# Eight small sums of a gated MLP's second pass, moved from VectorE to GpSimd

## The chip, the cores and the metric

The kernel runs on one core of a Trainium2 chip. Five engines work beside each other on that core: TensorE (PE in the profile) multiplies matrices, VectorE (DVE) and GpSimd (POOL) do sums of tiles, ScalarE (ACT) does copies, casts and the Gelu, and SyncE (SP) issues the transfers between HBM and the on-chip memory. Products are built up in eight banks of PSUM; POOL works only on SBUF here, so everything that reads a bank is DVE's or ACT's. The metric is the device time of one execution in microseconds (us), lower is better; several executions are timed, and their median counts.

## The reference

```
def reference(x, w_gate, w_up, w_down):
    g = jnp.einsum("bsd,df->bsf", x, w_gate)
    u = jnp.einsum("bsd,df->bsf", x, w_up)
    h = _gelu(g) * u
    return jnp.einsum("bsf,fd->bsd", h, w_down)
```

`_gelu` is the tanh form. x is 1 x 2048 x 1024, the two weights in front 1024 x 3584, the last 3584 x 1024, all in bf16.

## The kernel before

The 2048 rows of x are done in two passes (`ip` 0 and 1) of 1024 rows, which are two chunks of 512. A pass has two halves: the units, which make h from x, w_gate and w_up, and then `down` (line 515), which multiplies h by w_down.

**Units.** Each of the 14 units covers 256 columns of w_gate and w_up. A plain product would have eight blocks for each weight (two chunks of rows, two halves of the inner 1024, two halves of the 256 columns). The kernel does it in seven, by a scheme of Winograd's, with sums of blocks of x (`t1` to `t4`, four tiles each, with `tb` a cast; `make_t`, line 157) and sums of blocks of the weights (`s1` to `s4`, two tiles each; `make_s`, line 162). The sums of x are made once a pass, the sums of the weights for every unit. Two of the seven products need no sums and are called raw: `raw_products` (line 199) puts one into the banks `e`, copies it out with ACT (`p1`) and puts the other into the banks `c`. `finish_raw` (209) adds both on DVE (`add`, 204: first the gate part into a tile `sum`, then the up part in its bank), takes the Gelu on ACT, and multiplies the two on DVE into `hT`. The rest of a unit (`unit`, 213) is four products with sums, s2 by t2, s1 by t1, s3 by t3 and s4 by tb, and for units that are not `apart` a seventh, whole one (`whole_p4`).

**The divided product.** For pairs of units that `SPLIT` (line 47) names, the seventh product, with T4, is done for both units together, and the same scheme is applied to it once more (`split_p4`, 267). This needs sums of sums: `split_sums` (167) makes four tiles from the weights of both units, and `inner_sums_t` (256) makes n1 to n4 from the tiles of T4. Each n has two halves, so `inner_sums_t` issues eight instructions of 128 x 256, and they serve all divided pairs of a pass. In the first pass the first divided pair is units 4 and 5, and the n are made on GpSimd in unit 4 (`FIRST_N`, line 718). In the second pass it is units 0 and 1, and the n are first read at the end of unit 1.

**The boundary between the passes.** While the first pass's `down` runs, `more` (807) puts in the work that the second pass needs first, by steps: at step 50 the weights of units 0 and 1 are loaded, at step 58 DVE makes the sums of unit 0's weights, at step 62 it makes the sums of x and, behind them, the n. Then the second pass begins with the raw products of units 0 and 1, and both use the same pair of banks `K` for their second part, so unit 1's must wait until unit 0's has been read:

```
                raw_of(0, Ea, K)()
                raw_of(1, Eb, K)()
```

**What sets the order.** DVE, GpSimd, TensorE and SyncE do their work in the order in which the program names it (`manual_schedule`), in the units ScalarE too. An instruction that waits therefore holds all that stand behind it on its engine. Within a unit, `prepare` (713) is called behind the s1 product; it gives GpSimd its work: `split_sums` for the pair in its second unit, then the sums of the next unit's weights. Tiles of 2 KB a partition live in a pool of 52 slots (`SLOTS`); a new tile takes the slot that came free first, and the instruction that writes it waits until the former tile there has been read. Weights have three buffers of their own (`wpool`), so the load of unit u + 2 (`loaded`, called in `aside(0)`) waits until the last reader of unit u - 1's weights, among them `split_sums`, is done.

Of the kernel before, what the change touches and what calls it, by code (L numbers as in the profile page):

```python
# [10 lines left out]
def kernel(  # L11
# [60 lines left out]
    def slot(shape, dtype, name):  # L72
        return kpool.tile(shape, dtype, name=name, tag="k")
# [64 lines left out]
    def sums_s(w, eng):  # L138
        GU = range(2)
        sh = [P, KH, P]  # L140
        a11, a21 = [[w[:, i, :KH, h : h + P] for i in GU] for h in (0, P)]
        a12, a22 = [[w[:, i, KH:, h : h + P] for i in GU] for h in (0, P)]
        return Sums(
            how={
                "s1": lambda q, GU=GU: [new(eng, a21[i], a22[i], ADD, "s1", sh) for i in GU],
                "s2": lambda q: [new(eng, q["s1"][i], a11[i], SUB, "s2", sh) for i in GU],
                "s3": lambda q: [new(eng, a11[i], a21[i], SUB, "s3", sh) for i in GU],
                "s4": lambda q: [new(eng, a12[i], q["s2"][i], SUB, "s4", sh) for i in GU],
                "sa": lambda q: [cast(a22[i], "sa", sh) for i in GU],
                "sh": lambda q: cast(w[:, :, KH + 2 :, P:], "sh", [P, 2, 2, P]),  # L150
            }
        )
# [51 lines left out]
    def add(ps, other):  # L204
        g = new(dve, ps[0], other[0], ADD, "sum", dtype=f32)
        dve(ps[1], ps[1], other[1], ADD)
        return g, ps[1]
# [48 lines left out]
    def inner_sums_t(t, eng):  # L256
        n = t["n"] = [slot([P, 2, Q], f32r, "n") for _ in range(4)]
        left, right = slice(0, Q), slice(Q, N)
        for k in range(2):
            b1, b2 = t["t4"][k], t["t4"][2 + k]  # L260
            n1, n2, n3, n4 = [x[:, k] for x in n]
            eng(n1, b1[:, right], b1[:, left], SUB)
            eng(n2, b2[:, right], n1, SUB)
            eng(n3, b2[:, right], b1[:, right], SUB)
            eng(n4, b2[:, left], n2, SUB)
# [379 lines left out]
    s, t = sums_s(w, dve), sums_t(xT)  # L645
# [45 lines left out]
    def raw_of(u, e, c):  # L691
        p1 = raw_products(e, c, xT, loaded(u))
        return lambda: finish_raw(u, c, p1)

    def apart(u):
        return u - u % 2 in SPLIT[ip]

    for ip in range(NPASS):
        with tc.manual_schedule(engines={ENG.Activation}):
            if ip == 0:  # L700
                ws = {1: w, 2: ahead}
                late = lambda: add(cc, nxt["p1"])
            else:
                raw_of(0, Ea, K)()
                raw_of(1, Eb, K)()
            for u in range(1 if ip == 0 else 0, NU):
                js = making(u) if ip == 0 else []
                first = (ip, u) == (0, 1)
                odd_u = u % 2 == 1
                if first or not odd_u:  # L710
                    halves = {}

                def prepare():
                    if first:
                        pool_behind(t["t4"][-1])
                    if ip == 0 and (u >= NU - 2 or not apart(u)):
                        fetch_wd(making(u + 1))
                    if (ip, u) == (0, FIRST_N):
                        inner_sums_t(t, pool)
                    if odd_u and apart(u):  # L720
                        halves["sums"] = split_sums(ws[u - 1], ws[u])
                    if u + 1 < NU:
                        nxt["s"] = make_s(
                            loaded(u + 1), pool, () if apart(u) or apart(u + 1) else ("sa",)
                        )
                    if apart(u) and odd_u:
                        halves["sh"] = sums_s(ws[u], pool)["how"]["sh"](None)
                    if len(js) == 1:
                        store_made(js[0])
                    for j in js[1:]:  # L730
                        keep_whole(j)

                def keep(part, ps):
                    if js:
                        keep_part(js[0], part, ps)

                def aside(part):
                    if first and part < 0:
                        rest_of_0(part + 2)
                    if part == 0 and ip == 0 and apart(u) and u < NU - 2:  # L740
                        fetch_wd(making(u + 1))
                    if part == 0 and u + 2 < NU:
                        loaded(u + 2)
                    if part == 0 and "t4" not in t:
                        t.make("t4")
                    if part == 1:
                        if apart(u) and not odd_u and u + 1 < NU:
                            halves["sa"] = sums_s(ws[u], pool)["how"]["sa"](None)

                def mid():  # L750
                    if not apart(u) and "sa" not in s:
                        s.make("sa")

                def ahead():
                    if odd_u and u + 1 < NU:
                        raw_of(u + 1, Ea, D)()
                        nxt["c11"] = raw_of(u + 2, K, D)

                def behind():
                    if "c11" in nxt:  # L760
                        nxt.pop("c11")()

                def p4(c12):
                    if not (odd_u and apart(u)):
                        times(2 * u, 1, gelu(c12[0]), c12[1])
                    if first:
                        whole_p4(u, odd, s, t, after_first, behind)
                    elif not apart(u):
                        whole_p4(u, (Ea, Eb)[odd_u], s, t, ahead, behind)
                    elif odd_u:  # L770
                        rest = split_p4(
                            u - 1, Ea, Eb, *D, halves["sa"], halves["sh"], halves["sums"], t, c12
                        )
                        if u + 1 < NU:
                            p1 = raw_first(K, xT, loaded(u + 1)), raw_first(
                                D, xT, loaded(u + 2)
                            )
                            rest()
                            for n, c in enumerate((Ea, Eb)):
                                raw_second(c, xT, loaded(u + 1 + n))  # L780
                                finish_raw(u + 1 + n, c, p1[n])
                        else:
                            rest()

                def after_first():
                    raw_of(2, even, cc)()
                    nxt["c11"] = raw_of(3, dd, cc)

                if first:
                    banks = odd, cc, dd  # L790
                else:
                    banks = (Eb, D, K) if odd_u else (Ea, K, D)
                unit(
                    u, banks, s, t, late if first else None, prepare, aside, keep,
                    mid, p4,
                )
                if odd_u and not first and u + 1 < NU:
                    if not apart(u):
                        Ea, Eb, K, D = Ea, K, D, Eb
                    else:  # L800
                        Ea, Eb, K, D = K, D, Eb, Ea
                s = nxt.pop("s", None)

        last = ip == NPASS - 1
        got, nxt = {}, {}

        def more(step):
            if last:
                return
            if step in (-1, 0, 2):  # L810
                store_made({-1: NJ - 3, 0: NJ - 2, 2: NJ - 1}[step])
            if step == 0:
                xT[:] = new_x()
            if step >= 24 and step % 2 == 0 and step // 2 - 12 < len(moves):
                c, ko = moves[step // 2 - 12]
                transposing(xT, c, ko, (2 * (ip + 1) + c) * N)
            if step == 50:
                ws.clear()
                ws.update({n: load_w(n) for n in range(2)})
            if step == 58:  # L820
                got["s"] = make_s(ws[0], dve)
            if step == 62:
                got["t"] = make_t(xT)
                inner_sums_t(got["t"], dve)

        down(ip, Ea + D, K + Eb, last, more)
        Ea, Eb, K, D = K, Ea, Eb, D
        if not last:
            t, s = got["t"], got["s"]
# [29 lines left out]
```

## Time and profile before

| | us |
|---|---|
| median of three runs (541.38 to 542.25) | 542.18 |
| the profiled execution, its time | 542.75 |
| the profiled execution, its span | 541.0 |
| TensorE busy, share of the span | 98% |
| VectorE busy | 395.6 (73%) |
| GpSimd busy | 310.2 (57%) |
| ScalarE busy | 268.0 (50%) |
| eight n on VectorE, second pass (first start to last start) | 272.0 to 279.1 |
| eight n on GpSimd, first pass (first start to last start) | 57.7 to 62.8 |

All positions are microseconds from the span's start. The second pass begins near 271.7. In the profile nearly all sums of VectorE carry line 80 and those of GpSimd line 83, since two helpers record them; matmuls carry line 101. So one goes by the names of tiles: `n<-t` is an n made from T4. Matmuls are pipelined, so TensorE counts as busy also where it runs below its peak, and a row of the granted clock has to be read beside it. A bracket at the end of a line of the timeline gives the idle time of the engine just before, and what ended it.

### The profile page before, as it was taken

What the parts mean: (1) busy time and instruction counts of PE and PEld (TensorE: products, weight loads), DVE (VectorE), ACT (ScalarE), POOL (GpSimd) and SP (SyncE); (2) the same over time, 40 slices, a digit from 0 to 9 for tenths busy, and PEclk for the clock granted to TensorE, in tenths of its full rate; (3) what the DMA queues carried; (4) which work ended last, traced back from release to release, by engine and by line L of the source; (5) the groups of instructions that cost most, each with busy time, mean ns of one, the idle gap of its engine ahead of it and who ended that gap; (6) DMA issues with size and microseconds to landing.
All of it is one profiled execution on the core that took longest, in us unless ns stands there. A gap on an engine that the chain in (4) does not pass through costs nothing.

```text
span 541.0 us, 7973 instructions
## 1 busy us (share of the span) xinstructions
PE 531.6 (98%) x2550; PEld 387.7 (72%) x2571; DVE 395.6 (73%) x604; ACT 268.0 (50%) x479; POOL 310.2 (57%) x291
## 2 busy tenths in 40 slices
PE   8999999999999999999979999999999999999997
PEld 4568686868677646888838686867777685478887
DVE  2986777887887895695884857676766759979844
ACT  3557476767676410264335565566565561113340
POOL 1179999889898200000088898989898900000194
PEclk9999999999999999999989999999999999999999
DMA  9685556748483899979643250505052039662752
GB/s 243 161 219 171 181 156 194 225 127 264 129 266 126 288 390 316 265 182 274 225 118 84 72 138 19 157 1 155 8 150 59 22 110 386 223 233 84 241 172 69
DMA packets 108202, 93.34 MB, mean 173 GB/s; under 512 B 17280, under 2 KB 93056, under 8 KB 108160
## 3 DMA queue, kind: packets, MB, share of 16 engines
q1 hardware_dynamic: 108160, 92.82, 58.0%
q8 instruction: 21, 0.34, 0.3%
q14 instruction: 21, 0.17, 0.1%
HBM read 74.45 MB, written 15.20 MB: 166 GB/s over the span
## 4 chain that ended last, share of the span: by engine, by line
PE 93%; DMA 4%; DVE 2%; issue 1%; SPq 0%; DVEq 0%
PE bank L101 92%; DMA q<-td 2%; DVE n L80 1%; DMA xn<-in_x_dram 1%; DVE t L80 1%; DMA out_dram<-st 1%; SPq L587 0%; SPq L362 0%; DVE st L80 0%; PE bank L594 0%; DVE sum L80 0%; DVEq L80 0%; SPq L466 0%
## 5 line engine op out<-in xcount | busy, mean ns | idle before, releaser
L83 POOL TENSOR_TENSOR s<-w 128x512 fp32r<-128x512 bf16 x122 | 142.0, 1181 | 123.0 <-PE bank L101 103.2
L101 PE MATMUL bank<-t,s 128*128 128x512 f32 (+1 forms) x688 | 160.7, 387 | 0.0
L101 PEld LDWEIGHTS bank<-t,s 128*128 128x128 f32 x688 | 127.5, 188 | 26.7 <-issue 0.3
L101 PE MATMUL bank<-xT,w 128*128 128x512 bf16 (+1 forms) x489 | 110.3, 380 | 4.0 <-DVE sum L80 3.1
L179 ACT ACTIVATE g<-sum 128x512 f32<-128x512 f32 x101 | 63.9, 633 | 74.7 <-DVE sum L80 74.2
L80 DVE TENSOR_TENSOR hT<-g,bank 128x512 bf16<-128x512 f32 x112 | 76.6, 687 | 27.2 <-ACT g L179 20.5
L101 PEld LDWEIGHTS <-w 128*128 128x128 bf16 x504 | 48.5, 99 | 60.1 <-issue 5.8
L97 ACT COPY p<-bank 128x512 f32<-128x512 f32 x124 | 69.1, 588 | 39.2 <-PE bank L101 38.7
L83 POOL TENSOR_TENSOR s<-s,w 128x512 fp32r<-128x512 f32 x60 | 69.1, 1170 | 2.3 <-ACT g L179 1.4
L83 POOL TENSOR_TENSOR s<-w,s 128x512 fp32r<-128x512 bf16 x60 | 69.3, 1175 | 0.0
L80 DVE TENSOR_TENSOR sum<-bank,p 128x512 f32<-128x512 f32 x54 | 37.1, 687 | 41.1 <-PE bank L101 40.7
L83 POOL TENSOR_TENSOR q<-q 128x256 fp32r<-128x256 f32 x28 | 21.0, 781 | 78.7 <-DMA raw<-in_w_down_dram 77.5
L101 PE MATMUL bank<-q 128*128 128x512 f32 x240 | 58.9, 389 | 0.0
L101 PE MATMUL bank<-tb,s 128*128 128x512 f32 x216 | 53.7, 390 | 0.2
L101 PEld LDWEIGHTS bank<-q 128*128 128x128 f32 x240 | 45.0, 188 | 9.3
L101 PE MATMUL bank<-raw,hT 128*128 128x512 bf16 x218 | 48.4, 379 | 0.3
L92 ACT CAST tb<-raw 128x512 fp32r<-128x512 bf16 x28 | 17.1, 624 | 61.4 <-DMA raw<-in_w_down_dram 27.7
L101 PEld LDWEIGHTS bank<-tb,s 128*128 128x128 f32 x216 | 40.3, 188 | 9.5 <-POOL s L83 1.2
L80 DVE TENSOR_TENSOR q<-hT 128x512 fp32r<-128x512 bf16 x56 | 39.0, 696 | 5.6 <-PE bank L101 5.6
L97 ACT COPY u<-bank 128x512 f32<-128x512 f32 x62 | 34.1, 585 | 15.0 <-PE bank L101 15.0
L80 DVE TENSOR_TENSOR bank<-bank,p 128x512 f32<-128x512 f32 x54 | 37.5, 694 | 4.9 <-PE bank L101 4.3
L101 PEld LDWEIGHTS <-hT 128*128 128x128 bf16 x224 | 21.8, 98 | 26.5 <-issue 0.5
(77 smaller groups left out, 581.9 us busy)
## 6 DMA issues: line engine op xcount, KB each, us to landing
raw<-in_w_down_dram SPq DMA_DIRECT2D x76, 256.0 KB, 4.2
q<-td SPq DMA_DIRECT2D x60, 256.0 KB, 4.6
w<-in_w_gate_dram SPq DMA_DIRECT2D x27, 512.0 KB, 4.2
w<-in_w_up_dram SPq DMA_DIRECT2D x27, 512.0 KB, 5.4
td<-m SPq DMA_DIRECT2D x12, 768.0 KB, 5.4
w<-td SPq DMA_DIRECT2D x6, 1024.0 KB, 10.1
out_dram<-st SPq DMA_DIRECT2D x32, 128.0 KB, 1.7
td<-w SPq DMA_DIRECT2D x2, 768.0 KB, 6.3
```

Of the source, the lines that this page charges most:

```text
L80: nc.vector.tensor_tensor(out=out, in0=a, in1=b, op=op)
L83: nc.gpsimd.tensor_tensor(out=out, in0=a, in1=b, op=op)
L92: nc.scalar.copy(out=t, in_=src)
L97: nc.scalar.copy(out=t, in_=ps)
L101: nc.tensor.matmul(ps, lhsT=lhs, rhs=rhs, start=start, stop=stop, skip_group_check=True)
L179: nc.scalar.activation(g, src, ACT.Gelu_apprx_tanh)
```

## The change

The eight sums n of the second pass are issued in another place and on another engine. They are no longer given to VectorE at step 62 of the first `down`, behind the sums of x, but to GpSimd in unit 0 of the second pass, behind its sums of unit 1's weights. The instructions, their shapes and their operands stay the same, and so does the first pass.

```diff
@@ -723,6 +723,8 @@
                         nxt["s"] = make_s(
                             loaded(u + 1), pool, () if apart(u) or apart(u + 1) else ("sa",)
                         )
+                    if (ip, u) == (1, 0):
+                        inner_sums_t(t, pool)
                     if apart(u) and odd_u:
                         halves["sh"] = sums_s(ws[u], pool)["how"]["sh"](None)
                     if len(js) == 1:
@@ -821,7 +823,6 @@
                 got["s"] = make_s(ws[0], dve)
             if step == 62:
                 got["t"] = make_t(xT)
-                inner_sums_t(got["t"], dve)
```

## Prediction

> **What bounds the kernel now.** The page comes first: TensorE (PE) is busy 98% of the span and holds 93% of the chain that ended last. So only a place where PE stands still, or runs slower than it could, is worth anything. The chain in order of time shows where it leaves PE; its columns are start, length, what:
>
> ```profile
> 270.76 1.29 DVE t L80 x2
> 272.05 0.34 DVE n L80
> 272.42 5.15 DVE n L80 x4
> 277.59 1.32 DVE n L80 x2
> ...
> 279.52 0.61 DVE sum L80
> 280.17 21.76 PE bank L101 x101
> ```
>
> These are the eight n sums of the change, and one `sum` behind them that PE waits for. The timeline of the same stretch says what PE was doing, and for how long each n ran (start, length, engine, line, operation; idle time before it in brackets):
>
> ```profile
> 271.69 5.35 PE L101 MATMUL bank<-xT,w 128*128 128x512 bf16 x23
> ...
> 276.19 1.37 DVE L80 TENSOR_TENSOR n<-t 128x256 fp32r<-128x256 f32 x1
> 277.24 1.33 POOL L83 TENSOR_TENSOR s<-w 128x512 fp32r<-128x512 bf16 x1
> 277.59 1.25 DVE L80 TENSOR_TENSOR n<-t,n 128x256 fp32r<-128x256 f32 x1
> 278.77 0.41 DVE L80 TENSOR_TENSOR n<-t,t 128x256 fp32r<-128x256 f32 x1
> 279.11 0.41 DVE L80 TENSOR_TENSOR n<-t,n 128x256 fp32r<-128x256 f32 x1
> 279.44 0.68 DVE L80 TENSOR_TENSOR sum<-bank,p 128x512 f32<-128x512 f32 x1
> ...
> 280.17 3.49 PE L101 MATMUL bank<-xT,w 128*128 128x512 bf16 x8 [3.13 <-DVE sum L80]
> ...
> 283.10 6.14 PE L101 MATMUL bank<-t,s 128*128 128x512 f32 x24
> ```
>
> The 24 matmuls from 271.69 are unit 0's two raw products and unit 1's first. The next eight, unit 1's second product, write the banks K that `sum` (the first `add` of unit 0) and the product `hT` must read first. `sum` was ready when PE had filled the bank near 274.4, but stood in VectorE's (DVE's) queue behind the n sums until 279.44. An n takes 0.41 us when GpSimd (POOL) is still, and 1.25 to 1.37 while POOL makes unit 1's sums. The table by stretches shows what the stop does afterwards (length, then busy time of PE, PEld, DVE, ACT, POOL, then PE's granted clock, DMA share and GB/s):
>
> ```profile
> 277.00:280.20 3.20, 0.07 (x2) 0.03 (x1) 3.17 (x6) 0.05 (x1) 1.57 (x3) 1.00 0.63 159
> 280.20:283.70 3.50, 3.50 (x9) 1.56 (x9) 1.90 (x3) 2.17 (x4) 3.40 (x3) 0.51 0.02 5
> 283.70:290.00 6.30, 6.30 (x29) 5.15 (x29) 2.75 (x4) 3.18 (x6) 3.32 (x3) 1.00 0.00 0
> ```
>
> After standing still PE runs 3.5 us at half clock. Last, POOL's and PE's later rows, for what the moved work will meet:
>
> ```profile
> 281.31 2.29 POOL L83 TENSOR_TENSOR s<-w,s 128x512 fp32r<-128x512 bf16 x2
> 286.60 1.17 POOL L83 TENSOR_TENSOR s<-w 128x512 fp32r<-128x512 bf16 x1 [3.00 <-PE bank L101]
> ...
> 290.10 1.18 POOL L83 TENSOR_TENSOR s<-w,s 128x512 fp32r<-128x512 bf16 x1
> 291.24 2.30 POOL L83 TENSOR_TENSOR s<-w 128x512 fp32r<-128x512 bf16 x2
> ```
>
> **The change part by part.** *Removed from DVE: eight n sums,* 271.96 to 279.44, 7.5 us. What it is worth is read at PE, as three terms. (1) The stop: the last of the 24 matmuls starts at 276.66, and such matmuls start 0.21 us apart (32 of them from 301.54 to 308.27), so the next could start at 276.87 in place of 280.17: 3.30 us. (2) Eight at half clock: 280.17 to 283.10 is 2.93, at full clock 8 x 0.21 = 1.70: 1.23 us. (3) The start of unit 0's 24: 283.10 to the next group at 289.08 is 5.98, against 290.89 to 296.33 = 5.44 for the same 24 in unit 1: 0.54 us. Sum 5.07 us. Behind 289.08 the chain is PE without a break, so the gain keeps.
>
> [...]
>
> *What is late next on DVE.* `sum` needs K[0] (24 matmuls at 0.22: eight for the first product, four more, so 274.4) and its p1 copy (273.7). The t sums end at 272.05. Then `sum` 274.4 to 275.1, bank add to 276.0, Gelu beside it, `hT` to about 276.8. PE wants K[0] at 276.87 and K[1] four matmuls later, 277.72. From `sum`'s start to the end of `hT` took 279.44 to 281.52 = 2.08 us, so DVE may be free as late as 275.64 at no cost: 3.6 us of cover.
>
> *That cover can be eaten by POOL starting sooner.* POOL's first sum for unit 1 starts at 271.08, held until a PE matmul released a slot. The 52 slots are handed out as they come free, and n no longer takes four ahead of it. Two come free with each step of the last product (four matmuls; 56 from 258.99 in 12.85, so 0.92 us a step), so POOL can start up to two steps sooner, 269.24, while DVE still has its four t4 sums (269.56 to 272.05) to do. Bounds: none is delayed, as at 271.08, where the POOL sum took 2.32 and the t beside it 0.69 (free at 272.05); or each is delayed as n was (start to start 1.30 against 0.34, so 0.96 each), free at 272.05 + 3.84 = 275.89, which is 0.25 over the cover. I take none, the row where just these two kinds met: 0, at worst 0.25 us.
>
> *Added to POOL: eight n sums behind unit 1's eight.* Their row is from the first pass, where POOL did the same: 724 to 757 ns each, 57.68 to 63.44 with all gaps, 5.8 us. They issue no DMA. Behind them in POOL's queue stand the four sums of `split_sums`, then unit 2's eight; SP's load of unit 3's weights waits for the `split_sums`, as it overwrites unit 0's. Now the clock of POOL: unit 1's sums end by 273.2 + 7 x 1.16 = 281.3 (first one held to 273.2, the rest at 1.16 once DVE no longer uses two SBUF inputs beside it; 283.6 before). n to 287.1. `split_sums` 4.64 (286.60 to 291.24) to 291.7. Unit 2's, 9.1, to 300.8. What PE wants, 5.07 sooner than before:
>
> - n1 and split s1: first n matmul at 299.10, so 294.03; n has been there since 287.1, s1 is made by 288.3. Split s4: 300.10, so 295.03, made by 291.7. Slack 3.3 us or more.
> - Unit 2's first sums: 308.27, so 303.2; made by 296.3.
> - Unit 3's weights: first used by the raw products eight matmuls behind 301.54, so 298.15, the up half 299.0. The load was issued at 291.31, at the end of `split_sums`; now 291.7, with 4.0 (gate) and 5.3 (up, issued 0.4 later) to land, so 295.7 and 297.4. Slack 1.6 to 2.4 us, the thinnest of all. Unit 4's load now follows at once (unit 1's weights were released by a copy at 295.82, now near 290.8). The row for two such loads in a row beside other traffic (243.97) has 5.9 and 7.1: then 297.6 and 299.2, 0.2 late. I take 0, from the rows of this place; at worst 0.2.
>
> After that POOL gains on PE: in the pair from 350.53 it idles 0.78 + 1.39 of 24.85 us, so being some 5 us nearer to PE wears off in three pairs.
>
> *The sum:* -5.07 and nothing given back. The profiled execution took 542.75 (span 541.0), 0.57 above the median 542.18; 542.75 becomes 537.7, and the median 537.1, 0.94% less. With both worst ends, 0.25 + 0.2, it is 537.6.
>
> **The rivals.** *Part of the stop comes back.* If POOL starts early and DVE is delayed at all eight t3 and t4 sums, DVE is free at 272.05 + 8 x 0.96 = 279.7, and PE stands still as before. With five or six delayed it is free near 277.3, 1.7 late: gain 3.4 if the clock holds, 1.6 if a short stop halves it too; 538.8 to 540.6. For it: n was held like this. Against it: at 271.08 the t sums were not, and only four are left by 269.56. A middle case: each of the four t4 held for a whole POOL sum of 1.16 leaves DVE free at 276.7, 1.05 late, gain 4.0, 538.2; chance 0.08 of the 0.18 below. [...]
>
> *POOL becomes the bound, and the kernel slower.* Place: the first `split_sums` or unit 3's weights. It decides when `split_sums` end 3.3 us later than I have it (loads: 1.6), for example if slots are released to POOL only by PE's later reads. To end slower by 1.1 us, PE would have to stand 6.2 us, thus POOL to end at 301.2 in place of 291.7, or to lose 1 us in each of six pairs. For it: POOL waits on slots four times near here, and its idle share is small. Against: those waits (3.00 at 286.60) are POOL being ahead. 543.5 to 546.
>
> *The stop is not DVE's alone.* If `sum` had waited for something else as well, nothing would move: 542. Against it: its row has no idle time before it, and both its inputs were there five microseconds sooner.
>
> **How the numbers follow.** Full gain 0.72 (536.5 to 537.7); part comes back, at DVE or by late weights, 0.18 (538 to 540.6); no change 0.04; POOL the bound and slower 0.06. The time is that of the first, 537.1. The range takes the first and two thirds of the second: 536.4 to 539.4, 0.84. A change of 0.2% is 1.1 us, about what the spread of the runs (541.38 to 542.25) lets one tell: faster 0.90, same 0.04, slower 0.06.
>
> **What would show it.** Right: DVE's `sum` starts near 274.4 with idle time in front, waiting for PE; no gap at PE between the raw products; granted clock 1.00 from 277 to 290; eight n rows on POOL of 0.73 from about 281; the first n matmul near 294; POOL's 3.00 us wait at 286.60 gone. Wrong: t rows above 0.69 us on DVE, a POOL start before 269, a PE wait for POOL `s` or for the load of w near 294 to 299, or a half-clock stretch anywhere new.

## The result, and the profile after

The changed kernel takes 537.74 us (median of six runs, 537.28 to 538.24) against 542.1 us (six runs, 541.38 to 542.53): a ratio of 0.9922, 95% interval 0.9909 to 0.9934, so 4.4 us less. The profiled execution took 537.80 (span 535.9) against 542.75 (span 541.0): 5.0 less, 5.1 in the span.

The chain in order of time, which left TensorE between 251.0 and 280.2 us, now stays on it from 250 to 300 (start, length, what):

```profile
249.82 50.30 PE bank L101 x237
```

The timeline of the boundary after the change:

```profile
268.92 2.49 DVE L80 TENSOR_TENSOR t<-xT,t 128x512 fp32r<-128x512 bf16 x4
...
269.23 4.30 POOL L83 TENSOR_TENSOR s<-w 128x512 fp32r<-128x512 bf16 x2 [89.53 <-PE bank L101]
...
271.65 7.08 PE L101 MATMUL bank<-xT,w 128*128 128x512 bf16 x32
...
274.52 0.69 DVE L80 TENSOR_TENSOR sum<-bank,p 128x512 f32<-128x512 f32 x1 [3.12 <-PE bank L101]
...
278.38 5.82 PE L101 MATMUL bank<-t,s 128*128 128x512 f32 x24
...
280.21 0.74 POOL L83 TENSOR_TENSOR n<-t 128x256 fp32r<-128x256 f32 x1
...
284.03 1.98 PE L101 MATMUL bank<-tb,s 128*128 128x512 f32 x8
...
286.01 1.18 POOL L83 TENSOR_TENSOR s<-w 128x512 fp32r<-128x512 bf16 x1
...
290.65 2.29 POOL L83 TENSOR_TENSOR s<-w 128x512 fp32r<-128x512 bf16 x2
...
290.72 0.37 SPq L110 DMA_DIRECT2D w<-in_w_gate_dram  x1
...
294.05 1.17 PE L101 MATMUL bank<-n,s 128*128 128x256 f32 x8
```

All 32 raw matmuls stand in one row. `sum` starts at 274.52 and now it is DVE that waits for PE, 3.12 us, where PE waited 3.13 for DVE before. The eight n fill POOL from 280.21 to 286.01, `split_sums` end at 290.65, the load of unit 3's weights goes out at once, and the first n is read at 294.05. The table by stretches (length, then busy time of PE, PEld, DVE, ACT, POOL, then PE's granted clock, DMA share and GB/s); in the kernel before, the row from 280.20 had a clock of 0.51:

```profile
277.00:280.20 3.20, 3.20 (x17) 2.11 (x15) 1.95 (x3) 1.73 (x3) 3.20 (x3) 1.00 0.66 167
280.20:283.70 3.50, 3.50 (x17) 2.92 (x16) 0.43 (x2) 1.84 (x4) 3.42 (x6) 1.00 0.00 0
```

### The profile page after: what moved, and what is told of

Read it like the earlier page. It is cut to its first block, busy times and chain, and to the rows that moved or that the text cites. A ratio compares the mean times of both kernels' runs of the same rounds, so it can differ in the third digit from the quotient of the medians.

```text
span 535.9 us, 7999 instructions
## 1 busy us (share of the span) xinstructions
PE 530.7 (99%) x2571; PEld 387.4 (72%) x2571; DVE 388.2 (72%) x596; ACT 268.3 (50%) x479; POOL 315.7 (59%) x299
## 4 chain that ended last, share of the span: by engine, by line
PE 98%; DMA 1%; SPq 0%; DVE 0%; issue 0%
PE bank L101 98%; DMA xn<-in_x_dram 1%; SPq L587 0%; DVE st L80 0%; PE bank L594 0%
```

## The experiments

The theory: the gain is PE's stop between unit 1's raw products and the half clock behind it, and it comes from DVE's queue being free for `sum`; GpSimd hides the n. The rivals: DVE's load counts wherever it stands; GpSimd's queue has little room; the slow matmuls have a cause of their own.

**The place alone.** n stays on DVE, at the new place.

```diff
                     if (ip, u) == (1, 0):
-                        inner_sums_t(t, pool)
+                        inner_sums_t(t, dve)
```

> The n sums stay on VectorE but move to the new place, unit 0 behind unit 1's sums: the place alone, not the engine. Theory (the gain is VectorE's queue coming free for the first sum near 274.4): the raw products run on without a stop and the clock stays full, so the gain is that of the change, about 5 us less than before (ratio 0.991 to 0.993). In unit 0 VectorE is free from 280.3 to 283.4, and GpSimd ends unit 1's sums at 280.2, so eight sums of 0.34 to 0.41 should just fit, 283.1; if GpSimd's next sums slow the last ones, the next sum of a bank is up to 2 us late, which no matmul waits for. Rival (VectorE has to be rid of the 7.5 us, wherever they stand): the stop only moves into unit 0, and the ratio is 0.997 to 1.000.

Measured: 538.76 us against 541.85, ratio 0.9949 (0.9931 to 0.9967). The stop at the boundary is gone, but about a third of the gain is lost again. Both theories were too simple. DVE, POOL and PE in units 0 and 1 of this kernel:

```profile
280.76 0.42 DVE L80 TENSOR_TENSOR n<-t,n 128x256 fp32r<-128x256 f32 x1
...
280.94 1.26 POOL L83 TENSOR_TENSOR s<-w 128x512 fp32r<-128x512 bf16 x1 [1.25 <-PE bank L101]
...
281.09 1.39 DVE L80 TENSOR_TENSOR n<-t 128x256 fp32r<-128x256 f32 x1
...
285.22 2.88 PE L101 MATMUL bank<-t,s 128*128 128x512 f32 x12
...
286.33 0.68 DVE L80 TENSOR_TENSOR sum<-bank,p 128x512 f32<-128x512 f32 x1
...
288.46 1.21 PE L101 MATMUL bank<-t,s 128*128 128x512 f32 x4 [0.35 <-DVE hT L80]
...
290.34 2.08 PE L101 MATMUL bank<-t,s 128*128 128x512 f32 x8 [0.67 <-ACT u L97]
...
294.08 1.12 PE L101 MATMUL bank<-t,sa 128*128 128x256 f32 x8
```

Four n took 0.42 us. From 280.94 on POOL makes `split_sums`, and the other four take 1.27 to 1.39. So the next `sum` starts 15.30 us behind the first raw matmul (286.33, with that matmul at 271.03), where it is 11.75 in the changed kernel (283.40 and 271.65), and `hT` behind it ends too late for unit 1's s1 product, which writes the bank that `hT` reads. That product waits 0.35 us for `hT`, and the s3 product behind it 0.67 for a copy. I had expected no matmul to wait. Unit 1 takes 8.86 us (its first product at 285.22, the divided product at 294.08) in place of 7.25 (285.85 to 293.10).

**The engine alone.** n on GpSimd, at the old place, ahead of unit 1's sums.

```diff
                 got["t"] = make_t(xT)
-                inner_sums_t(got["t"], dve)
+                inner_sums_t(got["t"], pool)
```

> The n sums go to GpSimd but stay at the old place, ahead of GpSimd's sums for unit 1: the engine alone, not the place. Theory: the first sum on VectorE again starts near 274.4; n from about 271 to 277, unit 1's sums to about 286.3, of which s2 is wanted at 285.9 and made by 281.6, s4 is wanted at 291.3. Nothing stops: ratio 0.991 to 0.993. Rival (unit 1's sums become too late when they are put behind n, so the order within GpSimd's queue matters): TensorE waits for s at 285.9 by 1 us or more, ratio 0.994 or higher.

Measured: 537.04 against 541.85, ratio 0.9917 (0.9895 to 0.9939), as expected. The raw products run on in one row:

```profile
269.72 2.16 POOL L83 TENSOR_TENSOR n<-t 128x256 fp32r<-128x256 f32 x1 [90.76 <-DVE t L80]
...
270.91 7.08 PE L101 MATMUL bank<-xT,w 128*128 128x512 bf16 x31
...
276.86 2.28 POOL L83 TENSOR_TENSOR s<-w 128x512 fp32r<-128x512 bf16 x2
```

POOL has the eight n done by 276.86 and unit 1's sums by 285.85, and PE has no gap. Beside the change on another chip, to see whether this order is better:

> The kernel with n on GpSimd at the old place, ahead of unit 1's sums, once more beside the change on the same chip. Theory: TensorE has no stop in either, so both medians agree within 0.3 us. Rival (the order within GpSimd's queue is worth something, as 537.04 against 537.74 in two separate jobs hints): this one is faster by 0.5 us or more.

Measured: 537.57, ratio 0.9917 (0.9905 to 0.9928), against 537.41 for the change. The medians lie within the 0.3 us of the theory; the order within POOL's queue is worth nothing that can be told from these executions.

**The half clock by itself.** The kernel before, with PE kept at work through the stop by 14 matmuls of a constant into an idle bank.

```diff
-                raw_of(1, Eb, K)()
+                p1 = raw_first(Eb, xT, loaded(1))
+                for _ in range(14):
+                    matmul(D[0], warm[:, :P], warm, True, True)
+                raw_second(K, xT, loaded(1))
+                finish_raw(1, K, p1)
```

> The kernel before, with 14 matmuls of a constant into an idle bank of pair D put between the two raw products of unit 1, so that TensorE is at work through most of the stop; n stays where it was. They leave the output as it is. Theory (the stop costs 3.30 us by itself and 1.77 us by the half clock after it): the second product still starts at 280.17, but at full clock; 1.77 us less than before, ratio 0.9967. Rival (the slow matmuls behind the stop are due to something else, such as a late copy or weights, or the clock drops in the profiled execution only): no gain, ratio 0.999 to 1.001.

Measured: 540.66 against 541.85, ratio 0.9979 (0.9965 to 0.9992). Its timeline:

```profile
270.92 5.35 PE L101 MATMUL bank<-xT,w 128*128 128x512 bf16 x23
276.11 3.22 PE L101 MATMUL bank<-const-bfloat16-1.0 128*128 128x512 bf16 x14
279.17 1.98 PE L101 MATMUL bank<-xT,w 128*128 128x512 bf16 x8
280.81 5.83 PE L101 MATMUL bank<-t,s 128*128 128x512 f32 x24
286.48 1.98 PE L101 MATMUL bank<-tb,s 128*128 128x512 f32 x8
288.29 1.98 PE L101 MATMUL bank<-t,s 128*128 128x512 f32 x8
```

The eight matmuls behind the stop take 1.64 us from start to start in place of 2.93, the 24 behind them 5.67 in place of 5.98. From the first raw product to unit 1 it is 17.37 us in place of 19.20: 1.83 less, near the 1.77 forecast. Of this, 1.60 is the faster matmuls; 0.23 is the second product starting 8.25 us behind the first raw matmul in place of 8.48, which the sooner `sum` of this execution allowed. All twelve executions of this kernel show a mean granted clock of 0.999 or 1.0. So the slow matmuls come from PE having stood still. But the medians differ by 1.2 only. The executions listed with this run say why. Of 24 of the kernel before, seven show a mean granted clock of 0.999 or 1.0 and have a median of 540.40; seventeen show 0.994 to 0.997 and have 542.21, 1.81 more. The twelve of this kernel, with the clock held, have 540.66, close to the first group. In the profiled execution (0.996) the half clock behind the stop held for 3.41 us, which alone lowers the mean over 541 us by 0.003 (an estimate from these two lengths). So in some executions of the kernel before, the stop is followed by less half clock than that, or by none. Only one execution of it was traced, so how long its stop is in the others is not shown. The change was run again beside that:

> The changed kernel once more, beside the kernel before on the same chip, to split its gain. In 24 executions of the kernel before, 7 show a granted clock of 0.999 or 1.0 (median 540.4) and 17 one of 0.994 to 0.997 (median 542.1): the stop does not halve the clock every time. Theory: against executions with the clock held the change gains the stop alone, 3.3 us, against those with the half clock 5.1, and all its own executions show 0.999 or 1.0, at 537.0 to 537.4. Rival: the change gives some 0.6 us back somewhere, and its median stays at 537.7, 2.7 and 4.4 us below the two groups.

Measured: 537.41 (six executions from 536.93 to 538.25, and one at 542.46 with a clock of 0.997, which the theory does not have and which I can't explain), ratio 0.993 (0.9905 to 0.9955). On this chip ten executions of the kernel before with the low clock have a median of 542.14, two with the full clock 541.04 and 541.05. The change is 4.7 and 3.6 us below, where 5.1 and 3.3 were forecast. The 4.7 lies between the theory's 5.1 and the rival's 4.4, the 3.6 is nearer to the theory's 3.3 than to the rival's 2.7. With two executions in one group this speaks for two gains; it doesn't settle the last 0.4 us.

**GpSimd's room.** The n made twice over.

```diff
                     if (ip, u) == (1, 0):
                         inner_sums_t(t, pool)
+                        inner_sums_t(t, pool)
```

> The changed kernel with the eight n made twice over on GpSimd (the second time into four other tiles, which the products use): 5.8 us more in its queue. Tests the cover that the prediction gave GpSimd: 3.3 us at the divided product, 1.6 to 2.4 at unit 3's weights. In the profile after the change split_sums end at 290.7; here 296.5. Theory: TensorE waits for split s1, wanted at 294.05 and made at 293.0, not at all, for split s2 (wanted 294.5, made 294.2) hardly, for split s4 (wanted 295.06, made 296.5) 1.4 us, and then for unit 3's weights, issued 296.5 and landing at 300.5 and 301.8, wanted at 298.2 + 1.4: 1 to 2 us; 2 to 4 us slower than the change, ratio to before 0.995 to 0.999, and 1.8 more if a stop halves the clock. Rival (GpSimd has far more cover, it is only ever ahead): ratio 0.992 as the change.

Measured: 540.46 against 541.85, ratio 0.9981 (0.9967 to 0.9994), so 2.7 us slower than the change's 537.74 in the first set of executions, and 3.4 slower than the 537.04 of the engine alone, which ran beside it. PE's waits:

```profile
295.10 1.16 POOL L83 TENSOR_TENSOR s<-w,s 128x512 fp32r<-128x512 bf16 x1
...
296.29 0.37 SPq L110 DMA_DIRECT2D w<-in_w_gate_dram  x1
...
296.31 0.75 PE L101 MATMUL bank<-t,s 128*128 128x256 f32 x4 [1.39 <-POOL s L83]
...
300.22 1.04 PE L101 MATMUL bank<-xT,w 128*128 128x512 bf16 x4 [0.46 <-DMA w<-in_w_gate_dram]
...
302.03 4.27 PE L101 MATMUL bank<-xT,w 128*128 128x512 bf16 x19 [0.77 <-DMA w<-in_w_up_dram]
```

The wait for split s4 is 1.39 us, where 1.4 was expected, and the two for unit 3's weights, issued when `split_sums` ended, add 1.23: 2.62 us in all. The granted clock stays at 1.00 in every microsecond from 296 to 305: three short stops, none of which halves it. So the room on POOL is real and small, and the places are those that the prediction named.

**Half of the n left on DVE.** `inner_sums_t` takes the halves to make; the first half stays at step 62, the second goes to GpSimd.

```diff
-                        inner_sums_t(t, pool)
+                        inner_sums_t(t, pool, range(1, 2))
...
                 got["t"] = make_t(xT)
+                inner_sums_t(got["t"], dve, range(1))
```

> The change by halves: the four n of the first half stay on VectorE at the old place, the other four go to GpSimd at the new one. Tests the cover of 3.6 us that VectorE was given. From the rows of before, VectorE is then free at 276.2, the sum ends at 276.85 and hT at 278.3; TensorE wants the first bank at 276.87 and the second at 277.72. Theory: a stop of 0.3 to 0.9 us at the second bank, the clock holds, so 0.3 to 0.9 us slower than the change: ratio 0.992 to 0.994. Rival A (no cover is left, every microsecond of n on VectorE counts): half of the gain, ratio 0.995 to 0.997. Rival B (a short stop halves the clock too): 1.77 us more, ratio 0.996.

Measured: 537.28, ratio 0.9917 (0.9903 to 0.9931): the whole gain, and no stop at all.

```profile
270.95 7.08 PE L101 MATMUL bank<-xT,w 128*128 128x512 bf16 x31
...
273.57 1.37 DVE L80 TENSOR_TENSOR n<-t,n 128x256 fp32r<-128x256 f32 x1
...
274.87 0.68 DVE L80 TENSOR_TENSOR sum<-bank,p 128x512 f32<-128x512 f32 x1
```

The four n were slow, as before, and `sum` starts 3.92 us behind the first raw matmul. The cover was worked out to end at 275.64 - 271.69 = 3.95. The stop that I expected did not come because DVE's t sums ended 0.2 us ahead of the raw products in this execution and 0.4 behind them in the profile of before, where one of them had waited 0.58 for a store to free its slot. So the cover reaches at least to these 3.92 us, and half of the move is enough. That store's wait differs from execution to execution: it was 0.58 us in the profile of before and 0.60 in that of the engine alone, and is not there in the changed kernel; the t sums end 0.36 and 0.38 us behind the first raw matmul in the first two and 0.24 ahead of it in the third.

**The order of the n.** The kernel before, but n1, n3, n2, n4 with both halves of each in a row.

```diff
-        for k in range(2):
-            b1, b2 = t["t4"][k], t["t4"][2 + k]
-            n1, n2, n3, n4 = [x[:, k] for x in n]
-            eng(n1, b1[:, right], b1[:, left], SUB)
-            eng(n2, b2[:, right], n1, SUB)
...
+        two = [(t["t4"][k], t["t4"][2 + k], [x[:, k] for x in n]) for k in range(2)]
+        for b1, b2, m in two:
+            eng(m[0], b1[:, right], b1[:, left], SUB)
+        for b1, b2, m in two:
+            eng(m[2], b2[:, right], b1[:, right], SUB)
...
```

> The kernel before with the eight n on VectorE in another order: both halves of n1, both of n3, both of n2, both of n4, so that none needs the result of the one just ahead of it. Same engine, same place, same number. Theory (GpSimd gets between two VectorE sums only where VectorE has to wait for its own last result, as between the n; the t sums stand back to back and held the GpSimd sum for 2.32 us): the n take 0.34 to 0.42 us each, VectorE is free near 274.8, before 275.6, and the stop is gone with n on VectorE: ratio 0.991 to 0.993. Rival (the two engines take turns whatever the order, since each n has two inputs in SBUF): n 1.25 to 1.37 us each, and no gain, ratio 0.998 to 1.001.

Measured: 537.30, ratio 0.9909 (0.9897 to 0.9922). With n on DVE, at the old place, the whole gain is there.

```profile
271.75 5.36 POOL L83 TENSOR_TENSOR s<-w 128x512 fp32r<-128x512 bf16 x2 [91.34 <-DVE t L80]
...
272.21 0.75 DVE L80 TENSOR_TENSOR n<-t 128x256 fp32r<-128x256 f32 x2
...
272.88 0.75 DVE L80 TENSOR_TENSOR n<-t,t 128x256 fp32r<-128x256 f32 x2
...
273.56 1.43 DVE L80 TENSOR_TENSOR n<-t,n 128x256 fp32r<-128x256 f32 x4
...
275.23 0.69 DVE L80 TENSOR_TENSOR sum<-bank,p 128x512 f32<-128x512 f32 x1 [0.25 <-PE bank L101]
```

Eight n take 2.8 us, and now POOL is the one held: its first two sums take 5.36 us where two take 2.3 by themselves and took 3.61 in the kernel before. It is not a matter of when POOL begins: its first sum starts 0.46 us ahead of the first n here, and with the old order, where the n were held, 0.88 (the kernel before), 0.32 (half of the n) and 0.22 (the constant matmuls). Is it the order alone? Both edits together, the new order at the new place on DVE:

> Both edits together: the eight n on VectorE at the new place, in the order in which none needs the result just ahead. At the new place, in the old order, the first four n took 0.42 us and the last four 1.27 to 1.39, from the moment on when GpSimd came with its next sums; the fifth was held though it needs no earlier n. Theory 1 (a row of VectorE sums without a gap keeps GpSimd waiting, and the order alone decides): eight n of 0.42, done by 282.4, no stop in unit 1, 537.3 as the change, ratio 0.990 to 0.993. Theory 2 (the order mattered at the old place for another reason, for example that GpSimd's sum there was its first after a long rest; otherwise the two engines take turns): the n behind GpSimd's first sum are held again, 1.3 us each, and the ratio is 0.994 to 0.996.

Measured: 538.67, ratio 0.9953 (0.9917 to 0.9989). The ratio lies in theory 2's range, but the times don't decide between the theories: three of the ten executions show a clock of 0.993 to 0.997 and take 542.85 to 544.79, which I can't explain, and the other seven have a median of 537.69, near theory 1's 537.3. The trace speaks for theory 2: the last four n are held as soon as POOL begins, though the matmuls then wait only 0.22 us.

```profile
281.01 0.75 DVE L80 TENSOR_TENSOR n<-t,t 128x256 fp32r<-128x256 f32 x2
...
281.65 1.48 POOL L83 TENSOR_TENSOR s<-w 128x512 fp32r<-128x512 bf16 x1 [1.24 <-PE bank L101]
...
281.68 4.33 DVE L80 TENSOR_TENSOR n<-t,n 128x256 fp32r<-128x256 f32 x4
...
289.95 2.08 PE L101 MATMUL bank<-t,s 128*128 128x512 f32 x8 [0.22 <-ACT u L97]
```

So the order decides at the old place, where POOL's sum is its first after 91 us of rest, and not at the new one, where POOL had rested 1.24 us. Whether it is POOL's rest or something else at the old place that lets DVE keep ahead is not settled.

## Why the prediction was right

**The removed stop.** The three terms, 3.30 + 1.23 + 0.54 = 5.07, against 5.1 between the two profiled spans. From the first raw matmul to unit 0's tb product it was 289.08 - 271.69 = 17.39 us and is 284.03 - 271.65 = 12.38: 5.01. That the sum is so near is partly luck. Up to the start of unit 0's 24 matmuls the gain is 4.68 (11.41 less 6.73), where the first two terms give 4.53. The 24 themselves gain 0.33 and not 0.54: they take 5.65 us at full clock, not the 5.44 that was read from unit 1. That the stop came from DVE's queue and not from DVE's load as such is shown by the half left on DVE and by the new order: both leave n there and have the gain.

**The size in the median.** 537.74 was measured where 537.1 was forecast, 0.64 us more, within the range; the second set of the change gave 537.41. The forecast read two terms from one execution and took them for all. The first is the half clock, 1.23 + 0.54: over the three sets of runs whose clocks are listed, 11 of 49 executions of the kernel before kept the full clock. That puts the median of the kernel before 0.1 to 0.4 us below that of its executions with the low clock (542.01 against 542.14, 541.85 against 542.21). The second is the stop, 3.30: in the trace with the constant matmuls `sum` starts 7.08 us behind the first raw matmul, in the profile of before 7.75, so without them that stop would have been about 2.6 (an estimate from these starts). How much each has of the 0.64 is not shown, and the clocks of the six executions that the result compares with are not on record.

**The half clock.** The profile of before, by stretches (length, PE busy, granted clock):

```profile
280.00:280.20 0.20, 0.03 (x1) 1.00 0.00 0
280.20:280.40 0.20, 0.20 (x1) 0.71 0.00 0
280.40:280.60 0.20, 0.20 (x2) 0.50 0.00 0
...
283.60:283.80 0.20, 0.20 (x2) 0.76 0.00 0
283.80:284.00 0.20, 0.20 (x2) 1.00 0.00 0
```

The half clock holds from 280.28 to 283.70, 3.41 us. The clock record in that trace lists 276.480 us at full speed up to it, 3.413 at half and 256.000 at full behind it: 81, 1 and 75 steps of 3.413 us. Behind that, from 539.69 to the end of the span, it lists half speed again. In the trace of the changed kernel the stretch at full speed is 532.479 us, 156 such steps, and reaches past the last instruction. In the step ahead of the first half clock, 276.87 to 280.28, TensorE was busy for 0.28 us, so the stop lay almost wholly in one step; in the step ahead of the second, 536.28 to 539.69, it was busy for 1.40. Whether the place of the stop on these steps is how 11 executions kept the clock is not shown: no trace of such an execution is there. The forecast took the half clock from the rows of one execution: against executions with full clock the gain is about 3.4 (540.40 less the 537.04 of the engine alone, beside it) and 3.6.

**GpSimd's part.** n from 280.21 to 286.01, 5.80, as forecast from the first pass. `split_sums` ended at 290.65, forecast 291.7, a microsecond sooner because POOL began unit 1's sums sooner, at 269.23, forecast 269.24 at the earliest from four slots less ahead of it. PE read the first n at 294.05, forecast 294.03. That the room there is small was shown by the doubled n. POOL has idle time again at 345.49, in the third pair, as forecast.

**The rival of the slowed t sums** did not come true: four t4 beside POOL's sum took 2.49 us together, as ever, and POOL was held. The chance given to it stood on n being held, and the runs with another order show why that was a poor guide: the same n are not held at the same place when their order is changed. **POOL as the bound** needs 5.8 us more in its queue to cost about 3. **The stop not DVE's alone** is refuted by `sum` itself, which starts 4.9 us sooner and waits for PE.

One of my readings in the experiments failed outright: in the run with the place alone I took the bank sums of a unit for work that no matmul waits for, and the next unit's s1 product waited for the `hT` behind them.

## What to carry to other kernels

Price a stop of the bounding engine by its length and by what the clock does behind it, and look at the clock of several executions, since the second part may come in some only (here the low mean clock came in 38 of 49). Ask what instruction ends the stop and how late its queue may come free: here 7.5 us of sums had to lose about four (7.5 less the 3.6 of cover), and moving half, moving all or putting the same sums in another order all gave the same. Where the work goes, walk through the queue it joins: what stands behind it, which load waits for that, and when the result is wanted.

## What the runs showed that was not expected

- A stop of about 3.3 us of TensorE was followed by half a clock for 3.41 us. The mean clock is 0.994 to 0.997 in most executions of the kernel before (38 of 49) and not in all; the two groups are 1.8 us apart where there were enough of both to tell. Stops of 1.39, 0.46 and 0.77 us in six microseconds leave the clock at 1.00.
- A low mean clock is no proof of that stop: 5 of the 73 executions of the other kernels show 0.993 to 0.997 too, four of them at 542.46 to 544.79 us. None of the five was traced, and their cause is open.
- In these traces sums on VectorE with both inputs in SBUF and sums on GpSimd held each other, and which one was held changed: the first two GpSimd sums took 5.36 us, about 3 more than the 2.3 of two by themselves, beside eight VectorE sums that started after the first of them (the new order at the old place), and VectorE sums of 0.42 us took 1.27 to 1.39 when GpSimd came after a rest of 1.25 us (the place alone). Beside VectorE's sums from a bank a GpSimd sum took 1.16 us (280.20 in the profile of before), as it did with VectorE idle (1.16 at 287.85 there). What decides which one is held is not shown.
